# An attention and Fourier-mixing kernel: the first batch ordered by hand, w2 converted in the second batch, and the sequence DFT folded twice

## The chip, the cores and the metric

The kernel runs on one core of one Trainium2 chip. The metric is the device time of one execution in microseconds (us), lower is better. Before the change the median of three runs is 1923.09 us (1922.74 to 1923.3). The engines are TensorE (PE in the profile; PEld is its weight load), VectorE (DVE), ScalarE (ACT), GpSimd (POOL) and SyncE (SP), which issues most DMA transfers here. The inputs of the two weight matrices are float64, so the kernel makes float32 out of raw 64-bit patterns by itself.

## The reference, cut to what matters

```python
# batch, heads, seq, head_dim = 8, 8, 576, 64;  d_model = 512;  float32, weights float64
scores = scale * (q @ k^T)
thresh = max(scores, axis=-1) - tau                 # tau = 0.02
attn   = softmax(where(scores >= thresh, scores, -1e9))
x      = heads side by side of (attn @ v)           # (8, 576, 512)
mixed  = real(fft(fft(x, axis=1), axis=2))          # sequence, then channels
u      = x + mixed
un     = (u - mean(u)) / sqrt(var(u) + 1e-6)
out    = u + relu(un @ w_ch1) @ w_ch2               # 512 -> 2048 -> 512
```

## The kernel before

The program goes through 8 batches of 20 steps: four pairs of heads, five blocks of query rows each. Attention of batch b+1 is interleaved with the Fourier mixing and the channel layers of batch b; a scheduler decides the order on each engine. In the first batch there is no earlier batch to work on, so the weights are converted there, all 32 chunks of 128 x 512: 16 of w1 and 16 of w2.

```python
def load_weights(n, src, dst):                       # one chunk; DMA, then 4 DVE, 2 ACT, 1 POOL
    nc.sync.dma_start(out=raw, in_=src.bitcast(INT32))
    nc.vector.tensor_scalar(out=bits, in0=high, ...)                 # mantissa bits
    nc.scalar.activation(out=dst, in_=bits, func=ACT.Copy, ...)
    nc.vector.scalar_tensor_tensor(out=dst, in0=low, ...)            # low word added
    nc.vector.tensor_scalar(out=power, in0=high, ...)                # exponent by shift
    nc.scalar.activation(out=power, in_=power, func=ACT.Relu, ...)
    nc.vector.scalar_tensor_tensor(out=power, in0=high, ...)         # sign bit put in
    nc.gpsimd.tensor_tensor(out=dst, in0=dst, in1=power, op=ALU.mult)
...
def over_seq(y, table, rows, cols, m):               # DFT over the sequence, once folded
    for u in range(3):
        nc.tensor.matmul(pa[0:m, 0:KH], y[0:n, u, cols], table[0:n, u, :], ...)   # 289 columns
...
for i in range(total + 1):                           # one step = one block of query rows
    scores(i)                                        # scores, max, exp, mask, reciprocal
    fill()                                           # a piece of mixing and channel layers
    transposed_weights(i - 1)
    if t == 3: prep_pair(n + 1)                      # transposes of the next pair's q and k
    fill()
    if t == 0: weighted_values(n - 1)                # attn @ v, 40 matmuls; then the fold on POOL
    for _ in itertools.islice(chunks, 2): pass       # two weight chunks
    ...
    fill()
```

## Time and profile before

The prediction shows the lines of the page and of the stretches. The table only names them.

| stretch of the kernel before | length, us | PE busy | DVE busy | clock |
|---|---|---|---|---|
| first batch, first scores to last weighted values | 194.5 | 153.0 | 172.0 | 0.77 |
| its Fourier mixing, until channel matmuls run without a gap | 37.3 | 32.8 | 21.6 | 0.82 |
| from there to the end of the second batch | 131.2 | 131.0 | 69.9 | 1.00 |
| from there to the end | 1547.5 | 1526.3 | 605.8 | 1.00 |

### The profile page before, as it was taken

What the parts mean: (1) busy time and instruction counts of PE and PEld (TensorE: products, weight loads), DVE (VectorE), ACT (ScalarE), POOL (GpSimd) and SP (SyncE); (2) the same over time, 40 slices, a digit from 0 to 9 for tenths busy, and PEclk for the clock granted to TensorE, in tenths of its full rate; (3) what the DMA queues carried; (4) which work ended last, traced back from release to release, by engine and by line L of the source; (5) the groups of instructions that cost most, each with busy time, mean ns of one, the idle gap of its engine ahead of it and who ended that gap; (6) DMA issues with size and microseconds to landing.
All of it is one profiled execution on the core that took longest, in us unless ns stands there. A gap on an engine that the chain in (4) does not pass through costs nothing.

```text
span 1923.0 us, 20963 instructions
## 1 busy us (share of the span) xinstructions
PE 1845.8 (96%) x7840; PEld 992.8 (52%) x7840; DVE 870.4 (45%) x2015; ACT 612.5 (32%) x1110; POOL 236.9 (12%) x438
## 2 busy tenths in 40 slices
PE   6777899999999999999999999999999999999999
PEld 3444555455455455545555455545545445545454
DVE  6998555534333544544334444544434355431010
ACT  3555434333123334323223234322323233421010
POOL 3433110110000110011000020002000020001000
PEclk8876899999999999999999999999999999999999
DMA  5432100100000110100000010101000001000000
GB/s 150 129 113 77 32 19 14 37 24 13 18 22 22 30 25 14 31 24 13 18 24 19 18 31 13 31 24 25 13 23 19 24 19 25 1 11 6 11 6 16
DMA packets 129701, 56.97 MB, mean 30 GB/s; under 512 B 120677, under 2 KB 120678, under 8 KB 129600
## 3 DMA queue, kind: packets, MB, share of 16 engines
q1 hardware_dynamic: 129232, 54.71, 10.5%
q8 instruction: 62, 1.02, 0.2%
q0 software_dynamic: 368, 0.93, 0.2%
q14 instruction: 39, 0.32, 0.1%
HBM read 46.02 MB, written 9.44 MB: 29 GB/s over the span
## 4 chain that ended last, share of the span: by engine, by line
PE 86%; DVE 9%; ACT 1%; POOL 1%; issue 1%; SPq 0%; DMA 0%; DVEq 0%; ACTq 0%
PE po L582 26%; PE ph L561 25%; PE sc L319 10%; PE pv L409 7%; PE pw L387 6%; PE pa L491 3%; PE pt L296 2%; PE pv L416 2%; DVE neg L332 2%; PE py L474 2%; DVE e L345 2%; DVE stage L241 1%; PE pe L392 1%; PE pe L393 1%; DVE w L229 1%
## 5 line engine op out<-in xcount | busy, mean ns | idle before, releaser
L582 PE MATMUL po<-w,h 128*128 128x512 f32 x1152 | 537.3, 603 | 0.0
L561 PE MATMUL ph<-u_t,w 128*128 128x384 f32 x1536 | 528.7, 493 | 5.4 <-DVE h L569 3.3
L342 ACT ACTIVATE e<-sc,neg 128x576 f32<-128x576 f32 (+1 forms) x320 | 229.3, 740 | 582.3 <-DVE neg L332 579.4
L561 PEld LDWEIGHTS ph<-u_t,w 128*128 128x128 f32 x1536 | 280.7, 190 | 207.3 <-issue 22.5
L332 DVE TENSOR_REDUCE neg<-sc 128x1 f32<-128x576 f32 (+1 forms) x320 | 229.8, 750 | 328.3 <-PE sc L319 328.0
L582 PEld LDWEIGHTS po<-w,h 128*128 128x128 f32 x1152 | 204.4, 190 | 229.8 <-issue 224.4
L319 PE MATMUL sc<-kT,qT 64*128 64x288 f32 (+1 forms) x1280 | 260.2, 450 | 36.3 <-ACT e_t L390 19.1
L345 DVE SCALAR_TENSOR_TENSOR e<-sc,thr,e 128x576 f32<-128x576 f32 (+1 forms) x320 | 250.9, 814 | 30.3 <-ACT e L342 13.0
L319 PEld LDWEIGHTS sc<-kT,qT 64*128 64x128 f32 (+1 forms) x1280 | 128.5, 183 | 168.3 <-issue 99.6
L390 ACT COPY e_t<-pw 128x1024 f32<-128x1024 f32 (+1 forms) x160 | 148.3, 927 | 160.1 <-PE pw L387 154.8
L354 POOL COPY rec<-den 128x128 f32<-128x128 f32 (+1 forms) x160 | 50.0, 313 | 1105.0 <-DVE den L352 933.8
L387 PEld LDWEIGHTS pw<-ident,e 128*128 128x128 f32 (+1 forms) x1280 | 141.7, 146 | 72.3 <-issue 55.5
L387 PE MATMUL pw<-ident,e 128*128 128x128 f32 (+1 forms) x1280 | 168.7, 275 | 0.1
L567 ACT ACTIVATE h<-ph 128x384 f32<-128x384 f32 x96 | 47.2, 492 | 314.7 <-PE ph L561 314.7
L569 DVE TENSOR_SCALAR h<-ph 128x384 f32<-128x384 f32 x96 | 53.4, 556 | 185.1 <-PE ph L561 184.9
L420 DVE TENSOR_TENSOR x<-pv,ends 128x288 f32<-128x288 f32 x64 | 29.3, 457 | 192.1 <-PE pv L416 175.3
L589 DVE SCALAR_TENSOR_TENSOR u<-po,rstd,u 128x512 f32<-128x512 f32 x36 | 27.0, 750 | 157.1 <-PE po L582 157.1
L409 PE MATMUL pv<-e_t,v_in 128*64 128x288 f32 x512 | 72.5, 420 | 0.0
L409 PE MATMUL pv<-e_t,v_rev 128*64 128x288 f32 x512 | 71.8, 420 | 0.3
L394 ACT COPY ends<-pe 128x256 f32<-128x256 f32 (+1 forms) x160 | 57.1, 357 | 3.2 <-PE pe L393 3.2
L409 PEld LDWEIGHTS pv<-e_t,v_in 128*64 128x64 f32 x512 | 35.0, 139 | 38.0 <-issue 10.8
L409 PEld LDWEIGHTS pv<-e_t,v_rev 128*64 128x64 f32 x512 | 34.8, 139 | 37.6 <-issue 11.6
(98 smaller groups left out, 1266.4 us busy)
## 6 DMA issues: line engine op xcount, KB each, us to landing
stage<-in_moe_w_ch_dram SPq DMA_DIRECT2D x32, 512.0 KB, 4.0
out_dram<-u SPq DMA_DIRECT2D x36, 256.0 KB, 2.0
q_in<-in_q_dram SPq DMA_DIRECT2D x64, 128.0 KB, 2.4
v_in<-in_v_dram SPq DMA_DIRECT2D x64, 128.0 KB, 2.3
k_in<-in_k_dram SPq DMA_DIRECT2D x32, 128.0 KB, 2.4
k_in<-in_k_dram SPq DMA_DIRECT2D x64, 64.0 KB, 2.3
q_in<-in_q_dram SPq DMA_DIRECT2D x64, 16.0 KB, 2.2
k_in<-in_k_dram SPq DMA_DIRECT2D x64, 16.0 KB, 2.1
```

The source lines that it names most:

```text
L319: nc.tensor.matmul(sc[j][0:m, c, 0:HALF], qT[hp, 128 * t : 128 * t + m], kT[hp, HALF * c : HALF * (c + 1)], start=True, stop=True,)
L332: nc.vector.tensor_reduce(out=neg[0:m, j : j + 1], in_=sc[j][0:m, :, 0:HALF], axis=AXIS_XY, op=ALU.max, negate=True,)
L342: nc.scalar.activation(out=ej, in_=sc[j][0:m, :, 0:HALF], func=ACT.Exp, bias=neg[0:m, j : j + 1], scale=1.0)
L345: nc.vector.scalar_tensor_tensor(out=ej, in0=sc[j][0:m, :, 0:HALF], scalar=thr[0:m, j : j + 1], in1=ej, op0=ALU.is_ge, op1=ALU.mult, accum ...
L387: nc.tensor.transpose(pw[:, 4 * j + c, 0:m], e[0:m, c0 : c0 + 128], ident[0:m, 0:m])
L390: nc.scalar.copy(e_t[:, :, qs], pw[:, :, 0:m])
L394: nc.scalar.copy(ends[:, :, qs], pe[:, 0:2, 0:m])
L409: nc.tensor.matmul(pv[64 * j : 64 * j + 64, 0:HALF], vt[:, 2 * c + j, :], e_t[:, 4 * j + c, cols], start=(c == 0), stop=False, skip_group_ ...
L491: nc.tensor.matmul(pa[0:m, 0:KH], y[0:n, u, cols], table[0:n, u, :], start=(u == 0), stop=(u == 2),)
L561: nc.tensor.matmul(ph[:, 0:GT], w1[c][:, 128 * j : 128 * (j + 1)], u_t[:, c, c0 : c0 + GT], start=(c == 0), stop=(c == ND - 1),)
L569: nc.vector.tensor_relu(ht, ph[:, 0:GT])
L582: nc.tensor.matmul(po[:, :], hT[j // 4][:, j % 4, 128 * t : 128 * (t + 1)], w2[j][:, :], start=(j == 0), stop=(j == NJ - 1),)
```

## The change

Its intent is to shorten the first batch, where VectorE was the bound, and to take passes off TensorE elsewhere. Four things are done.

1. The first batch is ordered by hand (the program's order is taken as it is, no scheduler), the conversion of a chunk is cut into stages that are issued one per slot, the sign step leaves VectorE, and so do centering w1 and scaling q.
2. The w2 chunks are converted in the second batch, two in flight, through the half of the u buffer that is free then.
3. The sequence DFT is folded a second time: four matmuls of 144 or 145 columns in place of three of 289. The last 64 keys of the weighted values are padded to full height.
4. The last pair's fold goes to VectorE; table loads pass through the ring of score buffers; tau and the first pair's k come in on ScalarE's queue.

```diff
-    def load_weights(n, src, dst):
+    def convert(src, dst, raw):              # a generator: each yield is one slot
...
+        yield
         nc.scalar.activation(out=dst, in_=bits, func=ACT.Copy, bias=1.0, scale=2.0**-20)
+        yield
...
-        nc.vector.scalar_tensor_tensor(
-            out=power, in0=high, scalar=-(1 << 31), in1=power, ...)
-        nc.gpsimd.tensor_tensor(out=dst, in0=dst, in1=power.bitcast(FP32), op=ALU.mult)
+        nc.scalar.activation(out=sign, in_=high, func=ACT.Sign)
+        yield
+        nc.gpsimd.tensor_tensor(out=dst, in0=dst, in1=low.bitcast(FP32), op=ALU.mult)
+        nc.gpsimd.tensor_tensor(out=dst, in0=dst, in1=sign, op=ALU.mult)
...
+    def weights_2():
+        for j in range(NJ):
+            c = 2 * (j % 2)                  # two staging buffers inside u_t
+            raw = u_t[:, c : c + 2, S : S + WC].bitcast(INT32)
+            yield None, convert(w_ch2[128 * j : 128 * (j + 1), :], w2[j][:, :], raw)
...
-            for u in range(3):
-                nc.tensor.matmul(pa[0:m, 0:KH], y[0:n, u, cols], table[0:n, u, :], ...)
+            for parity, u, table, extra in ((0, 0, seq_even, seq_xe), (1, 2, seq_odd, seq_xo)):
+                at = pa[0:m, parity:KH:2]
+                nc.tensor.matmul(at, y[:, u, cols], table[:, odd, :], start=True, stop=False, ...)
+                nc.tensor.matmul(at, y[:, 1, cols], extra[:, odd, :], start=False, stop=True, ...)
...
-    def fill():
+    def fill(i):
+        if i > per_batch:
+            next(chunks_2, None)             # w2: two calls in each of three slots of a step
+            next(chunks_2, None)
...
+        if i == 7:
+            load_dim()                       # tables through the ring of score buffers
+            load_seq()
...
+    chunks_1 = run(weights_1(), STAGES)      # w1: six chunks in flight
+    chunks_2 = run(weights_2(), 2)           # w2: two
+    with tc.manual_schedule():
+        next(chunks_1)
+        prep_pair(0)
+        for i in range(per_batch + 1):
+            step(i)
+    for i in range(per_batch + 1, total + 1):
+        step(i)
```

## The prediction

> **What bounds the kernel now.** I read the page's slices first, then busy time in stretches that I chose by what the program is doing (first batch, its Fourier mixing, the rest), then the chain of waits, the list of groups and the timeline where a number was wanted.
>
> ```profile
> PE   6777899999999999999999999999999999999999
> ...
> DVE  6998555534333544544334444544434355431010
> ...
> PEclk8876899999999999999999999999999999999999
> ```
>
> Each digit is a tenth of busy time in 48 us. TensorE is not full, and its clock is not granted, in the first four to five slices; there VectorE is at nine tenths. From the sixth slice on TensorE is full. The stretches (columns: length, busy us of PE, PEld, DVE, ACT, POOL, then clock) say how sharply:
>
> ```profile
> 12.50:207.00 194.50, 152.99 (x618) 84.64 (x620) 171.95 (x372) 96.80 (x154) 63.91 (x66) 0.77 0.36 108
> 207.00:244.30 37.30, 32.76 (x147) 20.56 (x145) 21.58 (x49) 15.89 (x29) 10.98 (x19) 0.82 0.11 24
> 244.30:1923.00 1678.70, 1657.27 (x7068) 885.79 (x7068) 675.75 (x1590) 497.84 (x925) 155.37 (x330) 1.00 0.08 20
> ```
>
> So there are two regimes. From 12.5 us (first scores) to 207 us (last weighted values of batch 0) VectorE is 88% busy and TensorE runs at 0.77 of its clock. From 244.3 us, where the first channel matmuls run without a gap, TensorE is 98.7% busy at full clock for 1679 us. There only work taken off TensorE counts; before it, work taken off VectorE does.
>
> What fills VectorE in the first stretch is in the groups: the float64 weights, 32 chunks.
>
> ```profile
> L245 POOL TENSOR_TENSOR w<-w,stage 128x512 f32<-128x512 f32 x32 | 46.3, 1446 | 59.4 <-DVE stage L241 46.5 <-DVE den L352 12.9
> ...
> L241 DVE SCALAR_TENSOR_TENSOR stage<-stage 128x512 int32<-128x512 int32 x32 | 29.4, 918 | 0.0
> ...
> L234 DVE TENSOR_SCALAR stage<-stage 128x512 int32<-128x512 int32 x32 | 23.9, 748 | 0.0
> ...
> L229 DVE SCALAR_TENSOR_TENSOR w<-stage,w 128x512 f32<-128x512 uint32 x32 | 23.0, 717 | 0.8 <-ACT w L228 0.7
> ...
> L225 DVE TENSOR_SCALAR w<-stage 128x512 int32<-128x512 int32 x32 | 19.0, 594 | 0.4 <-DMA stage<-in_moe_w_ch_dram 0.4
> ```
>
> That is 0.92 + 0.75 + 0.72 + 0.59 = 2.98 us of VectorE per chunk, 95 us of its 172. For the second regime the timeline of TensorE shows two groups the change touches:
>
> ```profile
> 203.43 0.70 PE L416 MATMUL pv<-ends,v_in 64*64 64x288 f32 x4
> ...
> 226.57 1.92 PE L491 MATMUL pa<-seq_s,y_o 128*128 128x289 f32 x6
> ```
>
> Six instructions (three matmuls of two passes) of the sequence DFT hold TensorE 1.85 us start to start; four half-height ones for the last 64 keys 0.63 us.
>
> **What the Trainium skill says.** "TensorE: Matmul & The Clock Gate", Part 1: the clock is halved after about 3.4 us of an idle window and comes back after a busy one. The trace agrees: until 225 us the clock alternates between 1 and 0.5, mostly in steps of 10.2 us, 102 us at half rate in all; then it stays full. "TensorEngine Tiling (Array Packing)", Key Properties: changing the tiling mode drains TensorE. The trace agrees in size: a pass of 288 columns follows its predecessor by 243 ns within one mode and by 333 to 347 ns at a change. "SBUF — State Buffer", Who interferes with whom: VectorE and GpSimd share a port pair as an exclusive lock. The trace fits: the integer shift (L234) takes 0.42 us in the median and 0.75 in the mean, with single ones of 1.49 us while GpSimd multiplies.
>
> **The change part by part.**
>
> *First batch.* The 16 chunks of w2 leave it: 16 x 2.98 = 48 us off VectorE. The remaining 16 lose the sign step (L241, now a ScalarE Sign plus a second GpSimd multiply): 14.7 us. Centering w1 leaves VectorE for GpSimd and ScalarE: 10.3 us. Scaling q goes to ScalarE: 3.2 us. The last pair's fold and early sums come in: about 4 us. VectorE falls from 172 to 172 - 48 - 15 - 10 - 3 + 4 = 100 us, and I add 15 to 20 for a lock contended more often, since GpSimd does two 1.45 us multiplies per chunk: about 117. At today's 88% that is 133 us; with contention up to 142. TensorE rises: centering adds two matmuls a group (16 passes of 0.43 us, 6.9 us, four times), and batch 0's scores now go one head after the other, which the trace times at 2.04 us a step against 1.17 when heads alternate. Warm, 20 x (2.04 + 1.28 transposes) + 27 centering + 20 weighted values + 7 q/k transposes = 120 us. Neither engine alone is the bound any more; they wait for each other. Following one step: mask of head 0 ends, scores 1.25 us later, the maxima end 3.1 us after the mask, conversions 1.5 to 2.1, mask 0.8: 5.75 us. Twenty steps (four of them lighter) 109 us, centering overflow 4 x 4.8, weighted values 10, transposes 6, the five DFT table loads that now pass through the small ring of score buffers at step 8 about 8, half clock in places 8, drain 8: 168 us. The first way gives 142, this way 168, and the order was made by hand to hide such waits; I take 154. The start gains 3.4 us: tau no longer arrives last (11.4 us today) and k loads on a second queue, so scores start near 9.3. Last weighted values of batch 0: 163 instead of 207.
>
> *Mixing of batch 0*, 37 us today, is latency: fold, sums, six transforms limited by ScalarE copies, five sequence DFTs, GpSimd additions. New estimate: 6 + 7 + 6 + 1 + 6 = 26 to 27 us. Full channel work starts near 190.
>
> *From there.* The state differs: today 25 score steps and 6 pairs' transposes are done at 244, in the new order of instructions 23 and 5 at the first channel matmul, so 7.8 us of TensorE work is owed. The twice-folded DFT does 4 matmuls of 144 or 145 columns in place of 3 of 289, at full height: 8 passes of about 124 ns plus one change of mode, 1.19 us for 1.85: 0.66 x 5 x 7 batches = 23 us off TensorE. Zero-padded last keys at full height save two changes of mode, 0.15 us a half: 56 x 0.15 = 8.4 us. The w2 conversion now meets channel work in batch 1: over about 8 score steps VectorE has 29 us of attention, 16 x 2.06 = 33 of conversion, 7 of relu and statistics, 69 in all before contention, against 63 of TensorE work. I charge 12 us.
>
> Sum: 163 + 27 + 1678.7 + 7.8 - 23 - 8.4 + 12 = 1857 us, 3.4% faster.
>
> **Rivals.** *Hand order stalls.* In a fixed order every wait of one engine is every engine's; if steps take 7 us or more and the clock stays halved, batch 0 ends near 185 and the time is about 1879. For it: TensorE is only some 58% busy in an ordinary step, the level at which the clock alternates today. Against it: centering and weighted values now keep it warm. *w2 becomes the bound of batch 1.* GpSimd has 16 x 2.9 = 46 us of multiplies in those 69 us and shares VectorE's port; 25 us lost would give 1870. *Everything hidden.* If the conversions fall into gaps, batch 0 ends near 150 and w2 costs 3 us: about 1835. *The DFT saves nothing* if loading 128 stationary columns or stepped output limits short passes; today 64-column passes follow each other at 112 ns, so 124 is not far above that limit. That would give 1880.
>
> **Range and chances.** The first batch is uncertain by about 20 us either way, w2 by 10, the DFT by 8: in quadrature some 24; I narrow the lower end little and set 1832 to 1882. Slower would need the first batch to gain nothing. Two per cent is 1884.6; most rivals alone stay below it. Faster 0.91, same 0.085, slower 0.005.
>
> **What would show it.** Right: VectorE's busy time to the end of batch 0's weighted values near 117 us; that end near 163; clock above 0.85 there; first gapless channel matmuls near 190; sequence DFT about 1.2 us a call; no half-height passes in the weighted values; TensorE a few tenths below full for some 70 us in batch 1, then full. Wrong: DVE idle behind scores through batch 0, ScalarE's exponent at step 8 waiting 10 us or more for a table load, DFT passes at 240 ns, or gaps on TensorE behind masks long after 260 us.

## More of the kernel before

Busy time by stretch of the kernel before. Columns: the stretch, its length, busy us of PE, PEld, DVE, ACT and POOL with counts of instructions, then granted clock, DMA share and GB/s:

```profile
244.30:375.50 131.20, 131.00 (x667) 71.94 (x667) 69.93 (x170) 50.55 (x90) 11.50 (x30) 1.00 0.10 23
375.50:1923.00 1547.50, 1526.27 (x6404) 813.85 (x6402) 605.82 (x1420) 447.29 (x835) 143.87 (x300) 1.00 0.07 19
```

The reader is to see the second batch: TensorE is without a gap in it (131.0 of 131.2 us). Whatever is put there that makes TensorE wait costs its full length.

The chain that ended last, by engine, and the group of the first channel matmul, from the page of the kernel before:

```profile
PE 86%; DVE 9%; ACT 1%; POOL 1%; issue 1%; SPq 0%; DMA 0%; DVEq 0%; ACTq 0%
...
L561 PE MATMUL ph<-u_t,w 128*128 128x384 f32 x1536 | 528.7, 493 | 5.4 <-DVE h L569 3.3
```

The chain runs 86% of the time over TensorE; VectorE has the next share, 9% of 1923 us, 173 us, about what it is busy in the first batch (172.0 us). The channel matmuls lost only 5.4 us to waiting in the whole run.

## The result, and the profile after

The changed kernel takes 1946.57 us (median of 4 runs, 1945.51 to 1947.52). The kernel before, run beside it, takes 1923.19 us (4 runs). The ratio is 1.0121 with a 95% interval of 1.0103 to 1.0138: 1.2% slower.

The page's slices of the kernel after, in the same form as before:

```profile
PE   6678877999999999999999999999999999999999
...
DVE  5556465563334354553333354553333454441010
...
PEclk9778878999999999999999999999999999999999
```

VectorE fell from between six and nine tenths to five and six in the first four slices, as wanted. But TensorE and its clock now stay below full for seven slices, where it had been five. The stretches of the kernel after say it in microseconds: first batch, mixing, second batch until the last w2 multiply, rest of the second batch, all the rest.

```profile
12.50:204.70 192.20, 143.96 (x624) 84.85 (x622) 109.97 (x270) 90.53 (x150) 74.81 (x102) 0.80 0.26 73
204.70:236.70 32.00, 23.67 (x109) 16.16 (x110) 18.47 (x43) 10.04 (x20) 10.24 (x14) 0.82 0.05 11
236.70:336.00 99.30, 75.50 (x279) 41.80 (x277) 57.88 (x114) 54.62 (x96) 47.48 (x48) 0.78 0.29 89
336.00:421.40 85.40, 83.85 (x438) 46.66 (x437) 47.27 (x116) 33.53 (x56) 12.70 (x31) 1.00 0.11 25
421.40:1945.00 1523.60, 1498.40 (x6474) 829.11 (x6472) 605.12 (x1465) 458.28 (x858) 167.54 (x369) 1.00 0.08 20
```

In the first line VectorE has 62 us less work than before, and no engine is over 75% busy, but the stretch is hardly shorter: 192.2 us for 194.5. In the third, TensorE is at 76%, the others are below 60%, and the clock is 0.78; from the moment when the last w2 chunk is done (fourth line) TensorE is full at once. The last line is the largest gain, 1523.6 for 1547.5 us; the mixing gained 5 us (32.0 for 37.3). So the time went to two places: to the first batch, which should have been 40 us shorter, and to the second batch, which is 216.7 us from end to end of the weighted values (204.7 to 421.4) where it had been 168.6 (206.9 to 375.5).

The chain and the first channel matmul, from the page of the kernel after:

```profile
PE 82%; DVE 5%; POOL 5%; DMA 3%; issue 2%; ACT 2%; SPq 1%; DVEq 0%; POOLq 0%; ACTq 0%
...
L664 PE MATMUL ph<-u_t,w 128*128 128x384 f32 x1536 | 541.6, 501 | 26.0 <-ACT u_t L288 8.6
```

The chain hops between engines: GpSimd, DMA and ScalarE hold 10% together where they had 2%. The channel matmuls waited 26.0 us instead of 5.4; the largest part, 8.6 us, ended with ScalarE's part of a w2 conversion (the tile u_t at L288 is the sign step on the staging buffer). Section e9 comes back to this wait.

The w2 conversion by groups of instructions in the second batch (busy us, mean ns of one, idle before it and its releasers), to be read against the five groups in the prediction:

```profile
L291 POOL TENSOR_TENSOR w<-w,u_t 128x512 f32<-128x512 f32 x16 | 21.3, 1333 | 1.3
L290 POOL TENSOR_TENSOR w<-w,u_t 128x512 f32<-128x512 f32 x16 | 21.3, 1329 | 39.1 <-ACT u_t L284 35.8 <-DMA k_in<-in_k_dram 3.4
L274 DVE SCALAR_TENSOR_TENSOR w<-u_t,w 128x512 f32<-128x512 uint32 x16 | 13.0, 814 | 2.4 <-ACT w L272 2.4
...
L279 DVE TENSOR_SCALAR u_t<-u_t 128x512 int32<-128x512 int32 x16 | 10.7, 668 | 0.2
...
L272 ACT ACTIVATE w<-w 128x512 f32<-128x512 int32 x16 | 10.1, 630 | 19.8 <-DVE w L268 19.7
L268 DVE TENSOR_SCALAR w<-u_t 128x512 int32<-128x512 int32 x15 | 7.1, 471 | 26.1 <-DMA u_t<-in_moe_w_ch_dram 25.5 <-POOL u_t L616 0.6
```

VectorE's share of a chunk is 0.47 + 0.81 + 0.67 = 1.95 us, close to the 2.06 of the prediction: the work was counted right. What is new stands behind the last bar: VectorE idles 25.5 us in front of the first instruction for the chunk's load, ScalarE 19.7 us in front of the next for VectorE, GpSimd 35.8 us for ScalarE. Each engine takes its instructions in the order of its queue, so during such an idle time the attention's instructions behind it wait as well. The Trainium skill says so for three of them: "PSUM — Partial Sum Buffer", Engine vs sequencer instructions: "ScalarE/VectorE/GpSimdE queues are strict FIFO." The idle times in these groups agree.

The sequence DFT and the end of the weighted values on TensorE's timeline after (start, us, instruction, number of passes):

```profile
202.08 2.11 PE L486 MATMUL pv<-e_t,v_in 128*64 128x288 f32 x16
204.02 0.66 PE L486 MATMUL pv<-ends,v_in 128*64 128x288 f32 x4
...
453.82 0.41 PE L590 MATMUL pa<-seq_even,y_o 128*128 128x145 f32 x2
454.06 0.41 PE L594 MATMUL pa<-seq_xe,y_o 128*128 128x145 f32 x2
454.31 0.41 PE L590 MATMUL pa<-seq_odd,y_o 128*128 128x144 f32 x2
454.55 0.41 PE L594 MATMUL pa<-seq_xo,y_o 128*128 128x144 f32 x2
```

Each pair of DFT passes follows the other by 0.24 to 0.25 us, so 123 ns a pass, as estimated (124). The last keys now run at full height (128*64) like the rest.

The waits of the first batch after (engine, line, who released it, total us, times, longest; from the answers for VectorE, ScalarE, GpSimd and TensorE):

```profile
DVE neg L405 <- PE sc L391: 32.4, 22, 6.3
DVE x L491 <- PE pv L486: 14.7, 5, 8.3
DVE dim_c L224 <- DMA dim_raw<-in_dft_dim_dram: 12.3, 1, 12.3
DVE sums L534 <- POOL f L523: 8.7, 1, 8.7
...
ACT e L409 <- POOL seq_xe L208: 8.4, 1, 8.4
...
POOL half L510 <- DMA x<-swap: 15.0, 2, 7.7
...
PE pm L301 <- POOL w L291: 11.6, 3, 8.4
```

Beside the ordinary waits for scores there are single long ones. The table of the channel DFT keeps VectorE standing for 12.3 us, and a score buffer that a table load occupies holds ScalarE's exponent for 8.4 us. GpSimd stands twice, 15.0 us in all, before the fold of a swapped pair (a row exchange by DMA), with weight multiplies queued behind it, for which TensorE's centering waits 8.4 us at the longest. The 20 intervals between successive steps, read from the copies of the reciprocals in the trace, fall into three groups: eight of 5.2 to 6.3 us, near the 5.75 of the prediction, eight of 6.6 to 10.7, and four of 14.2, 19.6, 20.9 and 14.6 us.

### The profile page after: what moved, and what is told of

Read it like the earlier page. It is cut to its first block, busy times and chain, and to the rows that moved or that the text cites. A ratio compares the mean times of both kernels' runs of the same rounds, so it can differ in the third digit from the quotient of the medians.

```text
span 1945.6 us, 21474 instructions
## 1 busy us (share of the span) xinstructions
PE 1831.8 (94%) x7936; PEld 1022.9 (53%) x7936; DVE 841.0 (43%) x2017; ACT 650.0 (33%) x1182; POOL 316.8 (16%) x581
## 4 chain that ended last, share of the span: by engine, by line
PE 82%; DVE 5%; POOL 5%; DMA 3%; issue 2%; ACT 2%; SPq 1%; DVEq 0%; POOLq 0%; ACTq 0%
PE po L687 26%; PE ph L664 24%; PE sc L391 10%; PE pv L486 8%; PE pw L465 5%; PE pt L367 2%; DVE neg L405 2%; DMA u_t<-in_moe_w_ch_dram 1%; PE py L573 1%; POOL u_t L612 1%; DVE e L423 1%; POOL u_t L616 1%; POOL w L291 1%; PE pe L470 1%; PE pm L301 1%
## 5 line engine op out<-in xcount | busy, mean ns | idle before, releaser
L664 PE MATMUL ph<-u_t,w 128*128 128x384 f32 x1536 | 541.6, 501 | 26.0 <-ACT u_t L288 8.6
L687 PE MATMUL po<-w,hT 128*128 128x512 f32 x1152 | 536.1, 603 | 0.0
L687 PEld LDWEIGHTS po<-w,hT 128*128 128x128 f32 x1152 | 204.9, 190 | 228.5 <-issue 225.1
L391 PE MATMUL sc<-kT,qT 64*128 64x288 f32 (+1 forms) x1280 | 266.4, 456 | 29.9 <-DVE e L423 21.5
L423 DVE SCALAR_TENSOR_TENSOR e<-sc,thr,e 128x576 f32<-128x576 f32 (+1 forms) x320 | 250.6, 813 | 31.6 <-ACT e L409 15.5
L391 PEld LDWEIGHTS sc<-kT,qT 64*128 64x128 f32 (+1 forms) x1280 | 134.5, 185 | 149.6 <-issue 94.7
L670 ACT ACTIVATE hT<-ph 128x384 f32<-128x384 f32 x96 | 47.1, 491 | 330.7 <-PE ph L664 330.7
L672 DVE TENSOR_SCALAR hT<-ph 128x384 f32<-128x384 f32 x96 | 53.2, 555 | 218.9 <-PE ph L664 218.8
L510 POOL TENSOR_TENSOR half<-x 128x287 f32<-128x287 f32 x48 | 37.0, 791 | 111.4 <-DVE x L491 70.6
```

The costliest lines, as they stand in the source:

```text
L391: nc.tensor.matmul(sc[j][0:m, c, 0:HALF], qT[hp, 128 * t : 128 * t + m], kT[hp, HALF * c : HALF * (c + 1)], start=True, stop=True,)
L423: nc.vector.scalar_tensor_tensor(out=es[j], in0=sc[j][0:m, :, 0:HALF], scalar=thr[0:m, j : j + 1], in1=es[j], op0=ALU.is_ge, op1=ALU.mult, ...
L664: nc.tensor.matmul(ph[:, 0:GT], w1[c][:, 128 * j : 128 * (j + 1)], u_t[:, c, c0 : c0 + GT], start=(c == 0), stop=(c == ND - 1),)
L670: nc.scalar.activation(out=ht, in_=ph[:, 0:GT], func=ACT.Relu)
L672: nc.vector.tensor_relu(ht, ph[:, 0:GT])
L687: nc.tensor.matmul(po[:, :], hT[:, j, 128 * t : 128 * (t + 1)], w2[j][:, :], start=(j == 0), stop=(j == NJ - 1),)
```

## The experiments

Two theories stood after the first look. **Order and stalls**: the fixed order of the first batch turns single late arrivals (tables, fold) into waits of all engines, and w2 conversions in the second batch do the same; not the amount of work but where it stands in the queues is the cause. **Load**: w2 simply has to be done somewhere, costs VectorE and GpSimd what it costs, and the first batch is bound by the length of its chain.

In the table, "end of batch 1" and "batch 2" are from the profiled run: the time of the last weighted values of the first batch, and the time from there to those of the second. "Rest" is what follows. Each kernel was timed in 4 runs and is compared with the kernel before on the same chip (medians 1922.74 beside e1 to e4, 1923.72 beside e5 to e8, 1923.34 to 1923.43 beside the later ones).

| kernel | median us | ratio (95%) | end of batch 1 | batch 2 | rest |
|---|---|---|---|---|---|
| before | 1923.19 | 1 | 206.9 | 168.6 | 1547.5 |
| after | 1946.57 | 1.0121 (1.0103–1.0138) | 204.7 | 216.7 | 1524.2 |
| e1 no w2 conversion | 1896.3 | 0.986 (0.9845–0.9874) | 200.5 | 165.8 | 1528.4 |
| e2 w2 in first batch | 1953.76 | 1.0162 (1.0143–1.0182) | 258.0 | 168.2 | 1525.3 |
| e3 scheduler's order | 1921.83 | 0.999 (0.9975–1.0005) | 182.2 | 215.4 | 1524.2 |
| e4 scheduler, w2 first | 1894.03 | 0.9848 (0.9831–0.9866) | 203.6 | 161.9 | 1524.1 |
| e5 tables outside ring | 1942.81 | 1.0097 (1.008–1.0114) | 197.4 | 218.7 | 1529.6 |
| e6 late fold | 1940.13 | 1.0088 (1.0071–1.0105) | 192.1 | 217.8 | 1524.2 |
| e7 w2 faster calls | 1961.43 | 1.0198 (1.0183–1.0214) | 204.0 | 233.1 | 1525.6 |
| e8 w2 one buffer | 1976.04 | 1.0271 (1.0255–1.0286) | 203.3 | 244.8 | 1525.5 |
| e9 w2 half pace | 1921.69 | 0.9988 (0.997–1.0006) | 204.8 | 193.2 | 1523.5 |
| e10 w2 late touch | 1930.63 | 1.0036 (1.0018–1.0054) | 202.6 | 197.4 | 1528.6 |
| e11 both stalls out | 1932.54 | 1.0043 (1.0027–1.0059) | 186.2 | 217.3 | 1523.3 |
| e12 scheduler, stalls out, half pace | 1886.61 | 0.9803 (0.9785–0.982) | 170.3 | 191.8 | 1523.9 |
| e13 scheduler, stalls out, w2 first | 1889.09 | 0.9822 (0.9806–0.9837) | 200.7 | 163.7 | 1522.7 |

The rest differs by up to 7 us (1522.7 to 1529.6) among kernels whose later batches are the same program, and the end of the first batch by 4 us (200.5 to 204.8) among those whose first batch is. A profiled run is good for some 5 us and no more.

### e1: no w2 conversion

The w2 chunks are filled with a constant, so the output is wrong; everything else stays.

```diff
-            yield None, convert(w_ch2[128 * j : 128 * (j + 1), :], w2[j][:, :], raw)
+            nc.gpsimd.memset(w2[j][:, :], 0.01)
+            yield None, iter(())
```

> The changed kernel with w2 filled with a constant in place of loading and converting it (wrong result on purpose). Theory: the conversion of w2 in batch 1 is what costs most of the loss; from the first channel matmul to the end of batch 1 the changed kernel takes 46 us longer than the kernel before between the same points (375 to 421 us), so this kernel should take about 1946 - 46 = 1900 us (1890 to 1910). Rival: batch 1 is slow because of something else that the change did (folds on GpSimd, order of masks, one hT tile); then it stays above 1930 us.

Measured: 1896.3 us, as expected. The w2 conversion as placed costs 1946.57 - 1896.3 = 50 us, and all of it in the second batch (216.7 against 165.8 us). The stretch of the second batch in this run:

```profile
224.30:366.30 142.00, 138.44 (x727) 81.25 (x726) 79.10 (x193) 61.82 (x109) 22.98 (x55) 1.00 0.11 26
```

TensorE is busy 138 of 142 us at full clock. So the channel work in its new order was not the trouble.

### e2: w2 in the first batch, hand order kept

```diff
+        for j in range(NJ):                  # at the end of weights_1
+            yield None, convert(w_ch2[128 * j : 128 * (j + 1), :], w2[j][:, :], stage[:, n % STAGES])
...
             masks(i)
+            next(chunks_1, None)             # a second call in each step of the first batch
...
-    chunks_2 = run(weights_2(), 2)
+    chunks_2 = iter(())
```

> The changed kernel, hand order kept, with the 16 chunks of w2 back in the first batch behind w1, in the same six staging buffers, two calls of the conversion per step. Theory: the first batch is bound by waits in its fixed order and not by an engine's load (VectorE busy 110 of 192 us), so the extra 33 us of VectorE work there fit into gaps: batch 0 ends at 205 to 225 us instead of 204, batch 1 gains 46 us, total 1900 to 1920 us. Rival, the one of the prediction: load counts, batch 0 grows by 33 us or more and the total is 1930 or more.

Measured: 1953.76 us, a miss of my theory; the number lies where the rival, load, had put it (1930 or more). The second batch became clean (168.2 us), but the first grew to 258.0 us, 57 more than in e1. Its stretch:

```profile
12.50:258.00 245.50, 154.35 (x624) 87.39 (x623) 159.58 (x318) 118.68 (x198) 126.71 (x134) 0.74 0.29 87
```

VectorE is busy only 65% (159.6 of 245.5), so its load does not explain that number. Moving the chunks to where they had been before does not help by itself, because the hand order cannot take them.

### e3: the scheduler's order in the first batch

```diff
-    with tc.manual_schedule():
+    if True:
         next(chunks_1)
```

> The changed kernel without the hand-ordered block: the scheduler orders the first batch as it did before, w2 still in batch 1. Theory: the hand order is what leaves VectorE idle 82 of 192 us in the first batch, so the scheduler ends batch 0 earlier, at 160 to 190 us, and the total is 1905 to 1930. Rival: the waits come from the dependencies (buffers, table loads, swaps), and batch 0 still ends at 200 us or later, total 1940 or more.

Measured: 1921.83 us, as expected. The same instructions, ordered by the scheduler, end the first batch at 182.2 instead of 204.7 us. The hand order costs 22 us of the first batch.

```profile
12.50:182.20 169.70, 128.71 (x624) 77.43 (x623) 125.13 (x271) 93.00 (x150) 79.15 (x97) 0.85 0.29 82
```

VectorE's 125 us are 74% of the stretch here, where 110 us had been 57% by hand. The same instructions (271 for 270 counted) are thus 15 us longer on VectorE in this order; what lengthens them was not looked into. By the intervals between steps the scheduler did not remove the long step of the table loads (21.3 us for 19.6), but that of the second swapped pair fell from 20.9 to 7.4 us.

### e4: the scheduler's order, and w2 in the first batch

Both edits, of e2 and of e3.

> Both edits: scheduler's order and w2 in the first batch, that is the kernel before with the twice-folded DFT and the staged conversion. Theory: about 1880 to 1905 us, as batch 1 is free of w2 and each later batch gains about 3.8 us over the kernel before (1547.6 us from the end of batch 1 became 1524.6). Rival: if the two edits' gains are the same gain, it is no better than the better of the two alone.

Measured: 1894.03 us, as expected, and faster than both kernels. With the scheduler the 16 chunks of w2 lengthen the first batch by 203.6 - 182.2 = 21 us, and they cost nothing in the second. The same edit cost 53 us by hand (258.0 - 204.7).

```profile
12.50:203.60 191.10, 139.44 (x625) 79.16 (x623) 169.60 (x319) 120.18 (x198) 126.54 (x129) 0.82 0.37 112
```

VectorE is 89% busy: in this form it is the bound again, as in the kernel before.

### e5: tables outside the ring of score buffers

The five table loads go through free halves of the u buffer, spread over steps 2 to 11, in place of one block at step 7.

```diff
-            raw = sb.tile([128, 2 * KH], FP32, tag="e", name="seq_raw")
+                raw = u_t[:, 2 * (u % 2) + c, 0:KH]
...
-        if i == 7:
-            load_dim()
-            load_seq()
+        if i == 2:
+            fetch_seq((0, 1))
+        if i == 5:
+            place_seq((0, 1)); fetch_seq((2, 3))
+        if i == 8:
+            place_seq((2, 3)); fetch_dim()
+        if i == 11:
+            place_dim()
```

> The changed kernel, hand order kept, with the five DFT table loads brought through the unused half of the u buffer (fetched at steps 2, 5 and 8, copied at steps 5, 8 and 11) in place of the ring of score buffers at step 7. Theory: in the changed kernel ScalarE's first exponent of step 8 waits 8.4 us for a table copy and VectorE 12.3 us for a table load, and steps 7 to 8 take 19.7 us where about 6.5 are usual; without it batch 0 ends 10 to 14 us earlier (191 to 195 us), total 1932 to 1937. Rival: the stall hides other waits (conversion, clock) and the gain is under 4 us.

Measured: 1942.81 us, 4 us less than the changed kernel, where I had expected 10 or more; the rival had said under 4. The long step fell from 19.6 to 10.5 us, the end of the first batch by 7.3 us in the profiled run. That the rest of the stall lay beside other waits, as the rival has it, is argued.

### e6: the fold of a swapped pair one step later

```diff
         xs[b][p] = x
+        if b == 0 and p % 2:
+            late.append(lambda: fold(n, x))      # run at the end of the next step
+        else:
+            fold(n, x)
```

> The changed kernel, hand order kept, with GpSimd's fold of a pair whose rows are swapped by DMA put one step later in batch 0. Theory: GpSimd stands in its queue 15.0 us for the swaps (two waits), the second multiplies of w1 behind it, and TensorE 11.6 us behind those; VectorE's early sums 8.7 us. With the fold one step later batch 0 ends 8 to 14 us earlier, total 1932 to 1938. Rival: GpSimd is not on the path (it is 39% busy), gain under 3 us.

Measured: 1940.13 us (1935.85 to 1941.66), 6.4 us less, just outside the 1932 to 1938 expected. Two steps of 14.2 and 20.9 us became 7.6 and 9.1, and the first batch ended 12.6 us earlier in the profiled run, which was the fastest of the four (1935.85 us), so 12.6 is the upper end. The wait of GpSimd for the row exchange, with the weight multiplies behind it, was a real stall, and one that the prediction had not seen.

### e7: w2 in faster calls

Four calls of the w2 generator per slot in place of two; still two chunks in flight.

```diff
-            next(chunks_2, None)
-            next(chunks_2, None)
+            for _ in range(4):
+                next(chunks_2, None)
```

> The changed kernel with four calls of the w2 conversion per filling point in place of two, so that its instructions stand twice as dense in the engines' queues. Theory: the 51 us of w2 come from the round trip of two staging buffers (about 10.4 us a chunk by its own instructions, 8 rounds, a little over 100 us in the trace), which calls don't shorten: change within 10 us, either way. Rival: the calls' pace sets it; then batch 1 shortens by 20 us or more (total under 1927).

Measured: 1961.43 us, 15 us slower than the changed kernel, which neither theory had named. The last w2 multiply came 10 us earlier (325.9 against 335.9), but it cost more:

```profile
229.00:326.00 97.00, 49.49 (x145) 25.48 (x145) 47.60 (x87) 44.31 (x76) 48.28 (x44) 0.65 0.25 82
```

TensorE is busy 51% at a clock of 0.65, and no engine reaches 52%. More of the conversion's instructions stand in each stretch of the queues. Which wait grew is told under e9.

### e8: one staging buffer

```diff
-            c = 2 * (j % 2)
+            c = 0
...
-    chunks_2 = run(weights_2(), 2)
+    chunks_2 = run(weights_2(), 1)
```

> The changed kernel with one staging buffer for w2 in place of two, the same instructions and bytes. Theory of the round trip: 16 rounds in place of 8, so batch 1 grows by 50 to 90 us (total 1995 to 2035). Rival, engine load as in the prediction: the load is the same, total within 10 us of 1946.

Measured: 1976.04 us, 29 us slower than the changed kernel; I had expected 50 to 90, and the rival, load, no more than 10. The conversion itself grew by 77 us (last multiply at 413.0 against 335.9), so a chunk's round trip is (413 - 227) / 16 = 11.6 us, but the second batch by only 28 us: other work went on between. The length of the chunk's chain alone does not explain the loss.

### e9: w2 at half pace

The mirror of e7: one call per slot.

```diff
-            next(chunks_2, None)
-            next(chunks_2, None)
+            next(chunks_2, None)
```

> The changed kernel with one call of the w2 generator per slot in place of two, the mirror of e7: 16 chunks of two in flight then take some 17 of the 20 steps of the second batch in place of some 9. Theory (the w2 conversion costs time because instructions that wait for a load or for another engine stand at the head of in-order queues, with the attention's instructions behind them; fewer calls per step leave less of them standing): the last w2 multiply moves from 336 to 380 us or later, TensorE's clock in the second batch comes out above 0.90, and the total falls by 15 to 40 us, to 1907 to 1932. Rival (each chunk costs its some 3 us of path wherever it stands, 16 chunks some 50 us): total 1940 to 1952.

Measured: 1921.69 us, 25 us less, by taking one line out. The engines do exactly the same work. The stretch until the last w2 multiply, where the changed kernel had a clock of 0.78:

```profile
228.00:352.00 124.00, 104.21 (x490) 61.19 (x487) 89.04 (x183) 73.79 (x130) 60.91 (x69) 0.92 0.25 76
```

And VectorE's wait for the w2 loads in the second batch, 25.5 us before:

```profile
DVE w L268 <- DMA u_t<-in_moe_w_ch_dram: 14.7, 9, 2.6
```

The last multiply moved to 352.3 only, not to the 380 that I had expected: the steps themselves had become shorter. The clock was above the 0.90 named.

How the pace acts is to be looked for on TensorE, whose time in the second batch can be split into busy and idle. The table does it from the last weighted values of the first batch to those of the second; the passes are the same, 823 to 825 counted. The last column is the idle time before channel matmuls that ended with the sign step of a w2 chunk on ScalarE (L288).

| kernel | calls a slot | length, us | PE busy | PE idle | clock | idle until L288 |
|---|---|---|---|---|---|---|
| e1 | no conversion | 165.8 | 158.1 | 7.7 | 0.97 | 0 |
| e9 | 1 | 193.2 | 169.2 | 24.0 | 0.92 | 1.3 |
| after | 2 | 216.7 | 183.0 | 33.7 | 0.87 | 8.6 |
| e7 | 4 | 233.1 | 181.1 | 52.0 | 0.82 | 31.6 |

The waits of the last column in the changed kernel, in e9 and in e7:

```profile
PE ph L664 <- ACT u_t L288: 8.6, 3, 5.9
PE ph L664 <- ACT u_t L288: 1.3, 2, 0.9
PE ph L664 <- ACT u_t L288: 31.6, 3, 17.5
```

About half of the changed kernel's loss, 25 us, is that the same passes take longer at a lower clock; the other half is idle time. From the changed kernel to e7 the idle time grows by 18 us, and this one wait alone by 23. The idle times in front of the conversion's own instructions do not follow the loss: VectorE for the load, ScalarE for VectorE and GpSimd for ScalarE add up to 81 us in the changed kernel, and to 84 us both in e9 and in e7.

The wait for L288 is one that the data do not ask for: the sign step writes columns 576 to 1087 of u_t, and the channel matmuls of this batch read columns 0 to 383. The two share only the tile, because the staging buffers were put into the free half of u_t. Whether the program waits for that reason is not shown: no run has the w2 staging in a tile of its own.

### e10: w2 touched late

Four empty calls between the load and the first instruction of a chunk.

```diff
+            def apart(gen):
+                next(gen)                    # the load
+                for _ in range(4):
+                    yield
+                yield from gen
```

> The changed kernel with four empty calls between the issue of a w2 chunk's load and its first instruction on VectorE, so that the load has landed before an engine comes to it. Theory (head-of-line waiting): VectorE's waits for the w2 loads, 25.5 us in 13 waits before, fall to under 8 us, and the total falls by 10 us or more, to below 1937. If the waits vanish and the total stays at 1940 to 1952, the load's wait was hidden and the loss lies with the later links of the chunk's chain (ScalarE waiting for VectorE, GpSimd for ScalarE).

Measured: 1930.63 us, 16 us less. VectorE's wait for the loads fell from 25.5 to 15.0 us only (10 waits), not below 8. The total did what the theory said, the named wait only in part. Since e10 also spreads a chunk over more slots, it does not separate the wait for the load from the density of the other stages; TensorE's idle time until L288 fell too, from 8.6 to 1.7 us.

### e11: both stalls out, hand order kept

The edits of e5 and e6 together.

> The changed kernel, hand order kept, with both repairs: table loads outside the ring of score buffers (e5) and the fold of the swapped pairs one step later (e6). Theory (the hand order lost to the scheduler's by two kinds of stall that add up, 7 us and 13 us at the end of the first batch): the first batch's last weighted values end at 180 to 188 us, where the scheduler's order alone put them at 182, and the total comes to 1927 to 1936. Rival (both repairs uncover the same further wait): end of the first batch at 190 or later, total 1937 or more. Neither way is the 163 us of the prediction reached, which would need VectorE or TensorE near full.

Measured: 1932.54 us; first batch to 186.2 us, as expected. The two repairs add up at the end of the first batch: 7.3 + 12.6 = 19.9 against 18.5 measured. In the medians of the whole kernel the savings are smaller: 3.8, 6.4 and 14.0 us.

```profile
12.50:186.20 173.70, 135.21 (x625) 80.59 (x623) 107.48 (x270) 91.54 (x150) 74.85 (x102) 0.83 0.28 80
```

VectorE, at 107 us, is still only 62% busy. Two named stalls repaired bring the hand order near to where the scheduler was without any repair (182.2).

### e12: the scheduler's order, both stalls out, w2 at half pace

The edits of e3, e5, e6 and e9 together.

> The changed kernel with the scheduler's order in the first batch, table loads outside the ring, the late fold and w2 at half pace in the second batch. Theory (the missing time of the first batch is order and stalls, and the two add): the first batch ends at 163 to 174 us (182 with the scheduler alone, 186 with the repairs alone), the second takes some 193 us as with half pace, the total is 1880 to 1892. If the first batch stays at 178 or later, the repairs and the scheduler removed the same waits, and the 163 us of the prediction were out of reach of these data paths: total 1895 to 1905.

Measured: 1886.61 us (1883.55 to 1887.79), as expected and the fastest of all: 3.1% below the changed kernel and 2.0% below the kernel before. The output is correct.

```profile
12.50:170.30 157.80, 123.69 (x624) 74.04 (x622) 118.25 (x271) 92.51 (x150) 80.01 (x97) 0.89 0.31 89
```

The first batch ends at 170.3 us. Order alone had given 22.5 us and the repairs alone 18.5; together they give 34.4. So they are mostly two causes, with some 7 us in common.

### e13: the scheduler's order, both stalls out, w2 in the first batch

The edits of e2, e3, e5 and e6 together.

> The best kernel so far (scheduler's order, w2 in the first batch) with the two repairs added. VectorE was busy 89% of its first batch, so if VectorE bounds it there, the repairs save under 6 us and the total is 1886 to 1894; if the two stalls still lay on its path, they save 8 to 20 us, and the total is 1872 to 1885.

Measured: 1889.09 us. Against e4 (1894.03) the repairs bring 5 us, as expected if VectorE bounds this first batch:

```profile
12.50:200.70 188.20, 139.26 (x625) 78.52 (x623) 165.30 (x319) 120.00 (x198) 126.77 (x129) 0.80 0.38 114
```

VectorE is busy 88%, and stalls beside it matter little. Between e12 and e13 the intervals overlap. The four runs of e12 (at most 1887.79) all lie below those of e13 (at least 1887.96), but the medians differ by only 0.13%, so which place for w2 is better is not decided; both beat both kernels.

## Why the prediction was wrong

The number was 1857, the result 1946.57. The profiled span of 1945.6 us splits by the prediction's own milestones: first batch to 204.7 instead of 163 (+41.7), mixing 32.0 instead of 27 (+5.0), from gapless channel matmuls to the end of the second batch 184.7 us where the prediction's terms give 131.2 + 7.8 + 12 - 1.2 = 149.8 (+34.9), and the rest 1524.2 where they give 1547.5 - 23 - 7.2 = 1517.3 (+6.9); the 1.2 and 7.2 are one and six sevenths of the 8.4 us for padded keys. The sum is 88.5, the whole miss.

**VectorE's load: right.** Predicted about 117 us, measured 110: of the 15 to 20 us added for the shared lock some 10 came. There is luck in it, since the same instructions took 125 us in e3's order. **The start: right.** Scores start at 9.0 us, predicted 9.3, before 12.7.

**The length of the first batch: the step that failed.** It is "The first way gives 142, this way 168, and the order was made by hand to hide such waits; I take 154." Neither way was long enough (204.7 - 9.3 = 195), and choosing between them by the intent of the change was wrong. The ordinary step was right where it was undisturbed, 5.2 to 6.3 us for 5.75, but only eight of the 20 were. What failed is the list of exceptions. The table loads were on it with 8 us, and they measured 9 in their step and 7 at the end (e5), 4 in the median. The fold of the swapped pairs was not on it and cost up to 13 (e6), 6 in the median. And the hand order itself cost 22 against the scheduler's (e3), where it had been counted as a help. With all three taken away the first batch ends at 170 (e12), and 7 us to the 163 remain; the fourth long step, 14.6 us, is still 14.5 there and was not looked into. The low TensorE clock, 0.80 where above 0.85 was foretold, goes with this; in e12 it is 0.89. The level that the first rival names as the one where the clock alternates is in the trace of the kernel before: in the first batch TensorE was busy 81.1 us at full clock and 71.9 us at half, which as work at full clock is 81.1 + 36.0 = 117 of 194.5 us, 60%. The first rival, hand order stalls, had the right cause and too small a size (185). That the fixed order as such makes every wait everyone's is argued from the waits; shown is only that order and two stalls cost this much. Which reorderings of the scheduler are worth the 22 us stays open.

**The w2 conversion in the second batch: mis-sized, 12 us charged, 50 measured (e1).** The failing term is the charge of 12 us on the sum of VectorE work, "69 in all before contention, against 63 of TensorE work". Per chunk the work was right (1.95 us for 2.06). But the conversion was treated as load, and the loss is not load: e7, the changed kernel and e9 hold the same instructions with four, two and one call per slot, and the second batch takes 233, 217 and 193 us. Taken thinly, the conversion costs 27 us (193.2 - 165.8 of e1). What came in place of the sum is that TensorE stood idle 33.7 us instead of 7.7 and ran its passes at a clock of 0.87 instead of 0.97. The second rival had the right place and half the size (25 us), and named engine load as the cause, which no engine's busy time bears out. That the pace decides is shown; that waiting instructions at the heads of the queues are how it does so is argued, and the conversion's own idle times (81, 84 and 84 us) do not follow the loss. From the changed kernel to e7 the wait that grows is that of channel matmuls for the sign step, in the same tile; that the shared tile is its reason is a rival that no run tests. That the wait for the load is the largest part of it is not shown: e10 cut it only from 25.5 to 15.0 us, and spread the later stages too. What makes up the 27 us that remain at half pace is open too.

**Mixing: nearly right**, 5 us long. **The DFT: right.** TensorE's busy time in these matmuls after the second batch's end fell from 64.1 to 41.2 us for seven batches, 23 us as predicted. **The padded keys: right**, the weighted values fell from 133.3 to 124.4 us for six batches, 8.9 against 7.2. **The long regime** gained 23.3 us where DFT and keys give 30.2. The score passes in it grew from 172.2 to 178.9 us, as much as is missing, though TensorE's idle time grew too, from 21.2 to 25.2 us, and other passes became shorter by some 4. Number and shape of the score passes are unchanged, and changes of array mode fell from 645 to 538 as counted in the trace. What changed is how they stand: the eight passes of a step in one run take 1.2 us, and there are 80 such runs for 89; runs of four, with other matmuls between, take 1.01 us in the mean, and there are 42 for 24 (of 0.84). Why the order splits them more often stays open.

**The chances** followed from a width of 20 us for the first batch and 10 for w2. Both errors were larger and had the same sign, because both came from one habit: adding durations of work where waits decided. They were taken as independent.

## What to carry to other kernels

When no engine in a stretch is over about three quarters busy, work moved there need not be free: here its price hung on how densely its instructions were issued. Try the pace first, look for the waits of the critical engine that it lengthens, and be wary of a staging buffer inside a tile that the critical engine reads. The pace was worth 40 us here between the fastest and the slowest of three paces (1921.69 to 1961.43). Before ordering by hand, run the same instructions in the scheduler's order; and read the intervals between steps, not their mean: four of the 20 steps held 69 us here.

## What the Trainium skill lacked or had wrong

- "SBUF — State Buffer", Door 1: The DMA port swizzle, says that any non-contiguous access to PSUM significantly slows down matmuls. The twice-folded DFT writes every second column, and a float32 pass of 144 or 145 columns followed the other by 123 ns in the median, against 244 to 247 ns for 289 contiguous columns in the kernel before: no slowdown to be seen.
- "TensorE: Matmul & The Clock Gate", Part 1, gives the clock for idle and busy windows, and tells of short idle times that make it alternate, but gives no mean clock for a TensorE that is partly busy throughout. Here the mean clock was 0.65 at 51% busy (e7), 0.78 at 76% (after, second batch), 0.92 at 84% (e9) and 1.00 at 97% (e1); busy time is itself longer at a low clock (158.1 us at 0.97 in e1 and 183.0 at 0.87 after, for 823 passes).
- No page that I read gives what the pace costs at which side work is put into the engines' queues. Here one and the same conversion cost the second batch 27, 51 and 67 us at one, two and four calls per slot (e9, after, e7, each against e1), with no engine over 84% busy until the last w2 multiply.
